# One small operation moved from GpSimd to VectorE, and an activation table loaded earlier, in a fused attention and experts kernel

## The chip, the core and the metric

The kernel runs on one core of one Trainium2 chip. The metric is the device time of one execution in microseconds (us). A core has five engines that work side by side, each with a queue of its own that it works off in order: TensorE (PE, matrix products; PEld is its weight load), VectorE (DVE), ScalarE (ACT, functions from a table that is loaded in sets), GpSimd (POOL) and SyncE (SP, which issues most of the DMAs). An instruction waits at the head of its queue until the semaphores that it names are up, and all behind it wait with it.

## The reference, cut to what matters

Three parts run one after the other on 3072 tokens of 384 channels: a gated linear attention, a layer of eight experts of which each token takes at most one, and a gated feed-forward layer behind a root mean square.

```python
# attention, per batch and head, over t
state = f[t] * state + outer(k[t], v[t]);  y[t] = q[t] @ state
# experts: tokens with x @ w_skip > 0 only
h = np.maximum(xc[mask] @ w1[e], 0.0)
y[mask] = gate_w[mask, None] * (h @ w2[e])
out[do_compute] = xc + y
# gated feed-forward
rms = np.sqrt(np.mean(x * x, axis=-1, keepdims=True) + 1e-06)
xn = x / rms * rms_g
g = xn @ w_gate
silu = g * (1.0 / (1.0 + np.exp(-g)))
return (silu * (xn @ w_val)) @ w_out
```

## The kernel before, in words

**Numbers.** Products run in 16 bits: every operand is split into a high and a low part, and three products of parts are added in PSUM. The splits are made on the chip: ScalarE writes the high part (L390, L414), VectorE or GpSimd the low one (L391, L416). Activations carry a scale of 512 (`SX`).

**Stages.** Attention takes the first 180 us or so: 24 tiles of 128 tokens, each routed to its expert's rows in a DRAM table `xs` by an indirect scatter. Then come the eight experts, up to some 335 us. Expert `e` reads its 256 rows transposed, and for each of eight blocks `m` of the hidden layer makes nine products into PSUM (`products`, L993), the relu's high part on ScalarE (`hh`, L996) and its low part on VectorE (`hl`, L997), and, two blocks later (`LAG`), six products of the second layer (L1040). Last comes the gated layer: `pair` for the first two blocks of 512 tokens, `block` for the other four. Its `up` makes nine gate products (`pwg`) and nine value products (`pwv`, both L846), takes Silu of the gate on ScalarE (`sg`, L850) and multiplies on VectorE (`hf`, L852); `down` (L869) multiplies by the output weights.

**Side work in the expert stage.** Between the blocks of an expert run pieces of other work, dealt by `steps` out of two queues of generators: preparing the weights of the next experts (`prep1`, `prep2`) and of the gated layer (`prep_in`, with `narrow`, L190 to L197, which turns 64-bit values into 32-bit ones, then L409, L414, L416), and treating rows that leave the experts or skip them. The latter is what the change touches. `square` forms x2 from an expert's output and its input (L446 on VectorE and L447 on GpSimd, or L444 on GpSimd alone), lets ScalarE square it and sum the squares along the row (L451), then computes on GpSimd first mean plus epsilon (L452) and then its power -0.5 (L453), and scales the row by that: the high part on ScalarE (L457), the low part on VectorE (L458). `place` then scatters the row into the DRAM table `xnd` (L477, an indirect DMA that GpSimd issues); `first` transposes it straight into the input of the first two blocks. `square` runs 30 times: 16 tiles of expert rows, 6 of `middle` and 8 of `first`. Sums of squares also go into `ms_x`, from which `bounds` checks near the end that no row is too small (L930).

**Order.** The program fixes a priority for every instruction by where it is written; the order on each engine's queue is then made at build time by a planner that simulates the engines with modelled durations (`schedule_with_timeline_sim=True`). `tc.issue_after(a)` holds what is written in its block behind instruction `a` on the same engine. `pins` collects the two relu instructions of each block; `run` uses the newest of them to hold side work back. The tables of functions are loaded once at the start, for exponential and logarithm (L763), and once when the first Silu comes (L850); the second load is put there when the program is built.

The functions that the change touches, with the line numbers of the profile:

Of the kernel before, what the change touches and what calls it, by code (L numbers as in the profile page):

```python
# [13 lines left out]
AF = mybir.ActivationFunctionType  # L14
ALU = mybir.AluOpType
# [5 lines left out]
SX = 2.0 ** 9  # L21
# [62 lines left out]
def fused_kernel(ctx, tc, q, k, v, f, w_skip, w_gate, w1, w2, g_gate, g_val, g_out, rms_g, out, dbg=None):  # L84
    nc = tc.nc
    B, H, S, D = q.shape
    DM = H * D
# [42 lines left out]
    ms_x = keep.tile([128, 2 * E + MID + 2 * NB], F32, name="ms_x")  # L130
# [214 lines left out]
    def bank(i):  # L345
        return {"tag": "bt", "bufs": 2} if i in (1, 2) else {"tag": f"b{i}", "bufs": 1}
# [87 lines left out]
    def halves(t):  # L434
        return t[:, 0:DM].bitcast(F16)

    def parts(t):
        return halves(t).rearrange("p (a d) -> p a d", a=2)

    def square(xr, idx, y=None):  # L440

        x2 = nk.tile([128, DM], F32, tag="x2", name="x2")
        if y is None:
            nc.gpsimd.tensor_tensor(out=x2, in0=parts(xr)[:, 0, :], in1=parts(xr)[:, 1, :], op=ALU.add)  # L444
        else:
            nc.vector.scalar_tensor_tensor(out=x2, in0=y, scalar=xr[:, DM:DM + 1], in1=parts(xr)[:, 0, :], op0=ALU.mult, op1=ALU.add)  # L446
            nc.gpsimd.tensor_tensor(out=x2, in0=x2, in1=parts(xr)[:, 1, :], op=ALU.add)  # L447
        yield
        junk = nk.tile([128, DM], F32, tag="junk", name="junk", bufs=1)
        m = nk.tile([128, 3], F32, tag="m2", name="m2", bufs=4)  # L450
        nc.scalar.activation(out=junk, in_=x2, func=AF.Square, accum_out=m[:, 0:1])  # L451
        nc.gpsimd.tensor_scalar(out=m[:, 1:2], in0=m[:, 0:1], scalar1=1.0 / DM, scalar2=1e-6 * SX * SX, op0=ALU.mult, op1=ALU.add)  # L452
        nc.gpsimd.tensor_tensor(out=m[:, 2:3], in0=m[:, 1:2], in1=mhalf[:, 0:1], op=ALU.pow)  # L453
        yield
        xn = nk.tile([128, ROW], F32, tag="xn", name="xn")
        xp = parts(xn)
        nc.scalar.activation(out=xp[:, 0, :], in_=x2, func=AF.Copy, scale=m[:, 2:3])  # L457
        nc.vector.scalar_tensor_tensor(out=xp[:, 1, :], in0=x2, scalar=m[:, 2:3], in1=xp[:, 0, :], op0=ALU.mult, op1=ALU.subtract)  # L458
        yield
        return xn, m  # L460

    def place(xr, idx, y=None):

        xn, m = yield from square(xr, idx, y)
        mt = xr[:, DM:]
        if y is None:
            ms = m[:, 0:1]
        else:
            junk = nk.tile([128, DM], F32, tag="junk", name="junk", bufs=1)
            m3 = nk.tile([128, 1], F32, tag="m3", name="m3")  # L470
            nc.scalar.activation(out=junk, in_=parts(xr)[:, 0, :], func=AF.Square, accum_out=m3)
            ms = m3
        nc.vector.scalar_tensor_tensor(out=ms_x[:, idx:idx + 1], in0=mt[:, 1:2], scalar=0.0, in1=ms, op0=ALU.is_equal, op1=ALU.max)
        nc.vector.tensor_copy(out=xn[:, DM:], in_=mt)
        at = nk.tile([128, 1], I32, tag="at", name="at")
        nc.vector.tensor_scalar(out=at, in0=mt[:, 1:2], scalar1=float(NONE), scalar2=None, op0=ALU.add)
        sc = nc.gpsimd.indirect_dma_start(out=xnd, out_offset=bass.IndirectOffsetOnAxis(ap=at.bitcast(U32), axis=0), in_=xn, in_offset=None,  # L477
                                          bounds_check=NTOK - 1, oob_is_err=False)
        for o in places:
            tc.declare_no_dep(sc.ins, o, reason="the rows of two scatters differ")  # L480
        places.append(sc.ins)
        yield
# [432 lines left out]
    def bounds():  # L915
        NBIG = 2 + 2 * E + 3
        NC = 3 + NBIG
        NA = NC + 2 * E + 1
        bad = keep.tile([128, NC], F32, name="bad")
        vio = keep.tile([128, 4], F32, name="vio")  # L920
        tot = keep.tile([1, NA + NT], F32, name="tot")

        def worst(j, a, op, lim, red):

            nc.vector.tensor_reduce(out=vio[:, j:j + 1], in_=a, axis=AX.X if len(a.shape) == 2 else AX.XY, op=red)
            nc.vector.tensor_scalar(out=bad[:, j:j + 1], in0=vio[:, j:j + 1], scalar1=lim, scalar2=None, op0=op)

        worst(0, dec, ALU.is_le, DECAY, ALU.max)
        worst(1, ex_sum, ALU.is_le, EXPSUM, ALU.max)
        worst(2, ms_x, ALU.is_ge, 1.0, ALU.min)  # L930
        nc.vector.tensor_scalar(out=bad[:, 3:NC], in0=big, scalar1=TINY, scalar2=None, op0=ALU.is_ge)
        pt = ps.tile([128, 512], F32, **bank(3), name="tot")
        nc.tensor.matmul(pt[:, 0:NC], lhsT=onef, rhs=bad, start=True, stop=True)
        nc.tensor.matmul(pt[:, NC:NA], lhsT=ones, rhs=cnt, start=True, stop=True)

        def beyond(lo, hi, least, most=None):
            o, a = tot[:, lo:hi], pt[0:1, lo:hi]
            if most is None:
                nc.vector.tensor_scalar(out=o, in0=a, scalar1=least, scalar2=None, op0=ALU.is_lt)
            else:  # L940
                mid = (least + most) / 2.0
                nc.vector.tensor_scalar(out=o, in0=a, scalar1=-mid, scalar2=None, op0=ALU.add)
                nc.vector.tensor_tensor(out=o, in0=o, in1=o, op=ALU.mult)
                nc.vector.tensor_scalar(out=o, in0=o, scalar1=(most - mid) ** 2, scalar2=None, op0=ALU.is_gt)

        beyond(0, 3, 127.5)
        beyond(3, NC, 0.5)
        beyond(NC, NC + E, LOW, CAP)
        beyond(NC + E, NC + E + 1, NSK + 256, NSK + 128 * MID)
        beyond(NC + E + 1, NA, float(RA))  # L950
        return tot, NA
# [20 lines left out]
    pins = []  # L972
# [39 lines left out]
    def expert(e):  # L1012
        w2h, w2l = W[e][2:4]
        c0 = 0
        if e in ahead:
            xT, h = ahead.pop(e)
            c0 = RA
        else:
            xT = ek.tile([128, 2 * KD, CAP], F16, tag="exT", name="exT")
        rows(e, xT, c0, CAP, NT)  # L1020
        xr = nk.tile([128, CAP // 128, ROW], F32, tag="exr", name="exr", bufs=ERB)
        after(nc.sync.dma_start(out=xr, in_=xs[e * CAP:(e + 1) * CAP, :].rearrange("(t p) c -> p t c", p=128)), scatters)
        py = [ps.tile([128, DM], F32, **bank(4 + 2 * (e % 2) + t), name=f"ey{t}") for t in range(CAP // 128)]
        hs = {}

        def up(m):
            ph = ps.tile([128, 1, CAP - c0], F32, **bank(m % 4), name="ph")
            products(e, xT, ph, (m,), c0, CAP)
            if c0:
                hs[m] = [a[:, m, :] for a in h]  # L1030
            else:
                hs[m] = [ek.tile([128, CAP], F16, tag="h" + a, name="h" + a, bufs=LAG + 2) for a in "hl"]
            relu(hs[m][0][:, c0:CAP], hs[m][1][:, c0:CAP], ph[:, 0, :])

        def down(m):
            hh, hl = hs.pop(m)
            for t in range(CAP // 128):
                sl = slice(t * 128, (t + 1) * 128)
                for j, (a, w) in enumerate(((hh, w2h), (hh, w2l), (hl, w2h))):
                    nc.tensor.matmul(py[t], lhsT=a[:, sl], rhs=w[:, m, :], start=(m == 0 and j == 0), stop=(m == KF - 1 and j == 2))  # L1040

        for m in range(KF + LAG):
            if m < KF:
                up(m)
            if m >= LAG:
                down(m - LAG)
            yield
        for t in range(CAP // 128):
            add(place(xr[:, t, :], 2 * NB + MID + 2 * e + t, py[t]), ("y", e), 1)
# [24 lines left out]
    def run(main, n):  # L1074
        for _ in main:
            a, b = pins[-PIN]
            with tc.issue_after(a), tc.issue_after(b):
                for r in (0, 1):
                    steps(n[r], r)
# [19 lines left out]
    with m1x:  # L1099
        for e in range(E):  # L1100
            need("a", e)
            need("e", e)
            run(expert(e), N2)
            if e + WB < E:
                add(prep1(e + WB), ("a", e + WB))
                add(prep2(e + WB), ("e", e + WB))
            if e < MID:
                add(middle(e), ("mid", e), 1)
            if 2 <= e < 6:
                for t in (0, 1):  # L1110
                    a = 2 * (e - 2) + t
                    add(first(a // NB, a % NB), ("b", a // NB), 1)
        gates(0, 6)
# [58 lines left out]
```

## Time and profile before

| what | value |
|---|---|
| median of 3 runs | 774.69 us (773.26 to 774.88) |
| the profiled execution's own time | 774.52 us |
| its span, first to last instruction | 772.8 us |
| mean granted TensorE clock | 0.977 |
| busy: TensorE, VectorE, ScalarE, GpSimd | 719.5, 417.7, 362.7, 216.1 us |
| L451, squares of x2, ScalarE, x30 | 15.5 us, 518 ns each |
| L452, factor and epsilon, GpSimd, x30 | 13.8 us, 459 ns each |
| L453, power, GpSimd, x30 | 24.4 us, 814 ns each |
| table loads, ScalarE, x2 | 1283 ns each |

The profiled execution is 1.7 us longer than its span, which counts from the first instruction to the last. Durations are those of one execution. A row of a group gives line, engine, operation, output and inputs, shape and count, then busy time and mean duration, then how long the engine stood idle in front of these instructions and what ended that. An idle engine costs nothing unless the end of the kernel waits for it.

### The profile page before, as it was taken

How to read it: one execution, taken by the hardware profiler on the slowest of the kernel's cores; microseconds unless marked ns; L12 is line 12 of the kernel's file. 1: busy time of each engine (PE TensorE's matmuls, PEld its weight loads, DVE VectorE, ACT ScalarE, POOL GpSimd, SP SyncE). 2: the span in 40 equal slices, each digit the busy share in tenths (PEclk: the TensorE clock that was granted, in tenths of full speed). 3: DMA queues.
4: the chain of work that ended last, by engine and by line, in shares of the span. 5: the costliest groups of instructions: out<-in, count | busy, mean ns of one | idle time of the engine just before them, and what ended most of it. 6: DMA issues, size and time to landing. Idle time of an engine off the chain costs nothing.

```text
span 772.8 us, 14043 instructions
## 1 busy us (share of the span) xinstructions
PE 719.5 (93%) x5452; PEld 442.8 (57%) x5452; DVE 417.7 (54%) x879; ACT 362.7 (47%) x803; POOL 216.1 (28%) x286
## 2 busy tenths in 40 slices
PE   8999798995999888769999999999999999999995
PEld 5788687784776655534444566455455455555443
DVE  2788386885688888999999700222222222222230
ACT  5887477643577667778766410222312222123131
POOL 5221742442165565677320010200100020002002
PEclk9999899997999999999999999999999999999998
DMA  9999887844778998754332400100200030001001
GB/s 153 178 198 198 209 160 182 231 142 131 217 250 241 265 263 259 237 154 150 110 123 82 82 22 20 42 1 1 62 20 1 1 83 0 1 1 42 1 0 46
DMA packets 166459, 88.10 MB, mean 114 GB/s; under 512 B 137432, under 2 KB 151048, under 8 KB 166384
## 3 DMA queue, kind: packets, MB, share of 16 engines
q1 hardware_dynamic: 161904, 74.44, 39.9%
q0 software_dynamic: 4480, 12.67, 4.5%
q8 instruction: 45, 0.74, 0.4%
q14 instruction: 30, 0.25, 0.1%
HBM read 64.18 MB, written 16.24 MB: 104 GB/s over the span
## 4 chain that ended last, share of the span: by engine, by line
PE 67%; DVE 9%; DMA 8%; ACT 5%; POOL 4%; issue 4%; SPq 2%; POOLq 0%; ACTq 0%; DVEq 0%
PE po L869 18%; PE pwv L846 18%; PE pwg L846 18%; DMA st<-in_moe_w_dram 3%; PE py L641 2%; DMA xnd<-xn,at 2%; PE sc L625 2%; DVE w2l L391 2%; SPq L557 1%; PE py L636 1%; DVE w1l L391 1%; PE ptq L607 1%; DVE xn L458 1%; DVE hl L997 1%; DMA st<-in_moe_w_gate_dram 1%
## 5 line engine op out<-in xcount | busy, mean ns | idle before, releaser
L852 DVE SCALAR_TENSOR_TENSOR hf<-pwv,sg 128x512 f32<-128x512 f32 x72 | 49.5, 689 | 181.4 <-PE pwv L846 181.4
L877 POOL DMA_INDIRECT out_dram<-ot,ids x24 | 23.7, 988 | 336.8 <-ACT ot L876 332.3
L846 PE MATMUL pwg<-xnT,wgh 128*128 128x512 f16 x432 | 106.3, 382 | 7.5 <-ACT sg L850 7.5
L846 PE MATMUL pwv<-xnT,wvh 128*128 128x512 f16 x432 | 105.6, 379 | 0.0
L855 ACT CAST gh<-hf 128x512 f16<-128x512 f32 x72 | 44.3, 615 | 108.5 <-DVE hf L852 108.3
L869 PE MATMUL po<-wol,gh 128*128 128x384 f16 x288 | 93.7, 326 | 0.0
L869 PE MATMUL po<-woh,gh 128*128 128x384 f16 x288 | 93.7, 326 | 0.0
L869 PE MATMUL po<-woh,gl 128*128 128x384 f16 x288 | 93.4, 326 | 0.0
L850 ACT ACTIVATE sg<-pwg 128x512 f32<-128x512 f32 x72 | 42.5, 593 | 101.4 <-PE pwg L846 101.4
L869 PEld LDWEIGHTS <-gh 128*128 128x128 f16 x576 | 56.4, 98 | 41.8
L846 PEld LDWEIGHTS <-wgh 128*128 128x128 f16 x432 | 42.5, 98 | 55.4 <-issue 8.9
L856 DVE TENSOR_TENSOR gl<-hf,gh 128x512 f16<-128x512 f32 x72 | 52.6, 731 | 35.4 <-ACT gh L855 35.4
L846 PEld LDWEIGHTS <-wvh 128*128 128x128 f16 x432 | 42.3, 98 | 50.4 <-issue 0.3
L993 PE MATMUL ph<-exT,w1h 128*128 128x256 f16 (+1 forms) x384 | 57.3, 276 | 8.5 <-DMA exT<-xs 8.5
L846 PE MATMUL pwg<-xnT,wgl 128*128 128x512 f16 x216 | 59.3, 381 | 0.0
L846 PE MATMUL pwv<-xnT,wvl 128*128 128x512 f16 x216 | 58.7, 379 | 0.0
L993 PEld LDWEIGHTS <-w1h 128*128 128x128 f16 x432 | 40.6, 101 | 19.9 <-DMA exT<-xs 8.6
L1040 PE MATMUL ey<-w2h,hh 128*128 128x384 f16 x112 | 37.0, 331 | 7.1 <-ACT hh L996 7.1
L588 POOL TENSOR_TENSOR qs<-q,ep 128x384 f32<-128x384 f32 x24 | 26.8, 1117 | 56.3 <-ACT ep L584 38.5
L876 ACT ACTIVATE ot<-po 128x384 f32<-128x384 f32 x24 | 11.6, 489 | 58.2 <-PE po L869 50.9
L869 PEld LDWEIGHTS <-gl 128*128 128x128 f16 x288 | 28.2, 98 | 18.6
L1040 PE MATMUL ey<-w2h,hl 128*128 128x384 f16 x112 | 31.4, 332 | 7.1 <-DVE hl L997 5.2
(203 smaller groups left out, 1396.0 us busy)
## 6 DMA issues: line engine op xcount, KB each, us to landing
st<-in_moe_w_dram SPq DMA_DIRECT2D x32, 768.0 KB, 6.3
f<-in_f_logit_dram SPq DMA_DIRECT2D x24, 192.0 KB, 4.6
q<-in_q_dram SPq DMA_DIRECT2D x24, 192.0 KB, 4.0
k<-in_k_dram SPq DMA_DIRECT2D x24, 192.0 KB, 4.6
v<-in_v_dram SPq DMA_DIRECT2D x24, 192.0 KB, 4.4
st<-in_moe_w_gate_dram SPq DMA_DIRECT2D x6, 768.0 KB, 4.6
st<-in_moe_w_val_dram SPq DMA_DIRECT2D x6, 768.0 KB, 4.6
st<-in_moe_w_out_dram SPq DMA_DIRECT2D x6, 768.0 KB, 4.3
```

The costliest lines, as they stand in the source:

```text
L391: nc.vector.scalar_tensor_tensor(out=lo[:, :, sl], in0=src[:, :, sl], scalar=scale, in1=hi[:, :, sl], op0=ALU.mult, op1=ALU.subtract)
L588: nc.gpsimd.tensor_tensor(out=qs[:, :, 0:D], in0=ins["q"], in1=ep, op=ALU.mult)
L625: nc.tensor.matmul(scs[r][:, j, :], lhsT=T["k"][64 * r:64 * r + 64, j, :], rhs=T["q"][64 * r:64 * r + 64, j, :], start=True, stop=True)
L846: nc.tensor.matmul(p, lhsT=w, rhs=x, start=(j == 0), stop=(j == len(terms) - 1))
L850: nc.scalar.activation(out=sg, in_=pg, func=AF.Silu, scale=1.0 / SG)
L852: nc.vector.scalar_tensor_tensor(out=hf, in0=pv, scalar=SH / SG, in1=sg, op0=ALU.mult, op1=ALU.mult)
L855: nc.scalar.copy(out=hh, in_=hf)
L856: nc.vector.tensor_tensor(out=hl, in0=hf, in1=hh, op=ALU.subtract)
L869: nc.tensor.matmul(po[t], lhsT=a[:, sl], rhs=w, start=(m == 0 and j == 0), stop=(m == KF2 - 1 and j == 2))
L877: sc = nc.gpsimd.indirect_dma_start(out=out, out_offset=bass.IndirectOffsetOnAxis(ap=at[:, t:t + 1].bitcast(U32), axis=0), in_=ot, in_offs ...
L993: nc.tensor.matmul(out[:, i, :], lhsT=a, rhs=r, start=(j == 0), stop=(j == len(terms) - 1))
L1040: nc.tensor.matmul(py[t], lhsT=a[:, sl], rhs=w[:, m, :], start=(m == 0 and j == 0), stop=(m == KF - 1 and j == 2))
```

## The change

Four edits. The sum of squares is divided by the row length inside Square, by a scale of 384 to the power -0.5, here and in the second square that `place` makes for the check. What is left of L452, the addition of epsilon, goes to VectorE. The check's limit is divided by the row length. And the set of functions that holds Silu is loaded by hand, written behind expert one's work (`e == 0`) and held behind its last relu on ScalarE.

```diff
@@ square
-        nc.scalar.activation(out=junk, in_=x2, func=AF.Square, accum_out=m[:, 0:1])
-        nc.gpsimd.tensor_scalar(out=m[:, 1:2], in0=m[:, 0:1], scalar1=1.0 / DM, scalar2=1e-6 * SX * SX, op0=ALU.mult, op1=ALU.add)
+        nc.scalar.activation(out=junk, in_=x2, func=AF.Square, scale=DM ** -0.5, accum_out=m[:, 0:1])
+        nc.vector.tensor_scalar(out=m[:, 1:2], in0=m[:, 0:1], scalar1=1e-6 * SX * SX, scalar2=None, op0=ALU.add)
         nc.gpsimd.tensor_tensor(out=m[:, 2:3], in0=m[:, 1:2], in1=mhalf[:, 0:1], op=ALU.pow)
@@ place
-            nc.scalar.activation(out=junk, in_=parts(xr)[:, 0, :], func=AF.Square, accum_out=m3)
+            nc.scalar.activation(out=junk, in_=parts(xr)[:, 0, :], func=AF.Square, scale=DM ** -0.5, accum_out=m3)
@@ bounds
-        worst(2, ms_x, ALU.is_ge, 1.0, ALU.min)
+        worst(2, ms_x, ALU.is_ge, 1.0 / DM, ALU.min)
@@ the loop over experts
             run(expert(e), N2)
+            if e == 0:
+                with tc.issue_after(pins[-1][0]):
+                    nc.scalar.preload_act_table_set("silu_and_others")
             if e + WB < E:
                 add(prep1(e + WB), ("a", e + WB))
```

## The prediction

> **What bounds the kernel now.** I read the page first (span, TensorE's busy tenths), then busy time by stage, then TensorE's waits, the timelines around its longest one, and last the chain of waits that leads there.
>
> ```profile
> span 772.8 us, 14043 instructions
> PE   8999798995999888769999999999999999999995
> ```
>
> A digit of the second row is 19.3 us. From slice 19 on, about 360 us, TensorE is full until the last slice: there the gate and value products bound, and nothing the change touches is late. The holes that can be won or lost lie before. By stage:
>
> ```profile
> core 0: us, PE busy (x) PEld busy (x) DVE busy (x) ACT busy (x) POOL busy (x), PEclk, DMA share, GB/s
> 320.00:340.00 20.00, 17.31 (x107) 10.33 (x108) 19.92 (x32) 13.73 (x33) 16.97 (x15) 1.00 0.77 253
> 340.00:360.00 20.00, 12.56 (x51) 5.38 (x51) 18.22 (x30) 13.99 (x27) 15.10 (x16) 0.83 0.44 126
> ```
>
> Columns after the length: busy time of TensorE, its weight loads, VectorE, ScalarE, GpSimd. At the end of the expert stage VectorE is full (19.92 of 20), and TensorE waits. The table of waits of that stage (us in total, times, longest) names for whom:
>
> ```profile
> PE pwg L846 <- ACT sg L850: 7.5, 1, 7.5
> PE ey L1040 <- ACT hh L996: 7.1, 7, 2.3
> PE ey L1040 <- DVE hl L997: 5.2, 7, 2.4
> ```
>
> One wait of 7.5 us for the first gate function, and 14 of about one each for an expert's relu. The timelines, ScalarE's and then TensorE's, show the long one (start, us, engine, line):
>
> ```profile
> 343.16 0.51 ACT L409 ACTIVATE fb<-fb,gsc 128x256 f32<-128x256 f32 x1 [2.10 <-DVE fb L197]
> ...
> 344.88 0.60 ACT L457 ACTIVATE xn<-x,m 128x384 f16<-128x384 f32 x1
> 345.49 1.28 ACT L850 ACT_TABLE_LOAD   x1
> 346.79 0.60 ACT L850 ACTIVATE sg<-pwg 128x512 f32<-128x512 f32 x1
> ```
> ```profile
> 347.44 1.01 PE L846 MATMUL pwg<-xnT,wgh 128*128 128x512 f16 x2 [7.53 <-ACT sg L850]
> ```
>
> sg's row has no bracket, so it waited for nothing but its place in ScalarE's queue: behind weight and row work (L409, L457), and last behind the table load. It ends at 347.39 and TensorE starts 0.05 us later. So this load is on the path, whole.
>
> **The change, part by part.** The profiled execution took 774.52 us, 1.72 over its span, beside a median of 774.69 for the runs shown; the sum is made against 774.52.
>
> *The table load moved.* Gone from between 345.49 and 346.79: -1.28 us. By the order in the program it comes behind expert one's last relu:
>
> ```profile
> 201.24 0.30 ACT L996 ACTIVATE eah<-ph 128x160 f16<-128x160 f32 x1 [1.29 <-PE ph L993]
> 201.44 1.57 ACT L390 ACTIVATE w2h<-st 128x768 f16<-128x768 f32 x2
> 204.17 0.38 ACT L996 ACTIVATE hh<-ph 128x256 f16<-128x256 f32 x1 [1.17 <-PE ph L993]
> ```
>
> ```profile
> 200.00:220.00 20.00, 20.00 (x156) 14.66 (x155) 15.33 (x37) 14.29 (x32) 9.61 (x12) 1.00 0.67 202
> ```
>
> There two weight splits are queued behind it and then expert two's first relu, in front of which ScalarE idles 1.17 us: the load fits but for 0.1 us, and TensorE, 20.00 busy of 20 in this stretch, consumes that relu only two blocks of products later. I take 0; without that cover it is 1.28 again, at most. What is late next at the gate is TensorE's need for VectorE, 18.22 busy of 20 in that stage, but VectorE's own products there wait on the same ScalarE queue, so I let the whole 1.28 through; the bounds are 0 and 1.28. The Trainium skill, "ScalarE: Activation LUTs", section "What ACT_TABLE_LOAD costs", gives a switch 1283 ns and about 1380 ns of drain. The load agrees; no drain shows (the operation before ends at 345.48, sg starts at 346.79), and by the page's 2.66 the total would be 772.3.
>
> *The add moved from GpSimd to VectorE, the division into Square's scale.* Square with a constant other than one costs nothing by these two rows of 128x512, the first with a scale and the second without:
>
> ```profile
> L645 ACT ACTIVATE xT<-py 128x512 f16<-128x512 f32 x24 | 14.1, 586 | 1.1 <-PE py L641 1.0
> L610 ACT COPY Tq<-ptq 128x512 f32<-128x512 f32 x24 | 14.0, 585 | 6.2 <-PE ptq L607 6.1
> ```
>
> The limit in the bounds check is a constant, 0 too. The 30 GpSimd operations of L452 go. Most of their time is beside other work: GpSimd waits for ScalarE before them. What counts are those on the chain from 188 to 348 us, five pieces:
>
> ```profile
> L452 POOL TENSOR_SCALAR m<-m x30: 190/394/1222, 207.9 to 362.2; 128x1 f32<-128x1 f32 x30
> ```
> ```profile
> 214.56 0.80 POOL m L452
> ...
> 331.73 0.38 POOL m L452
> ```
>
> With 0.19, 0.27 and 0.80 between these two, together 2.44 us. In their place come five adds on VectorE. The trace has none; the nearest rows are a tensor_scalar of the same size and a copy of four elements; the other two are what such an add would find running:
>
> ```profile
> L476 DVE TENSOR_SCALAR at<-exr x16: 136/142/155, 207.1 to 360.8; 128x1 int32<-128x1 f32 x16
> ```
> ```profile
> L474 DVE COPY xn<-exr 128x4 f32<-128x4 f32 x16 | 6.4, 398 | 1.8 <-DMA xnT<-xn 1.8
> ```
> ```profile
> L997 DVE SCALAR_TENSOR_TENSOR hl<-ph,hh 128x256 f16<-128x256 f32 x56 | 22.9, 415 | 2.1 <-ACT hh L996 2.0
> ```
> ```profile
> L391 DVE SCALAR_TENSOR_TENSOR w2l<-st,w2h 128x768 f16<-128x768 f32 x27 | 28.5, 1074 | 5.3 <-ACT w2h L390 5.2
> ```
>
> An add takes 142 to 398 ns; I take 142, the same operation at the same size: 5 x 0.142 = 0.71. Each may find VectorE in the middle of something: nothing at best, a whole weight split of 1.07 us at worst; I take half of one relu's low part, 0.2 each, 1.0 together. So this term is -2.44 + 0.71 + 1.0 = -0.73, between -2.44 + 0.71 = -1.73 and -2.44 + 5 x (0.398 + 1.074) = +4.9. The Trainium skill, "Advanced Engine Details and Errata", section "VectorE Performance Modes", says that GpSimd's instructions and two-port VectorE ones block each other, and counts tensor_scalar among those with such a mode: a rule against this move. The rows bear it out for wider ones (below), but the 16 of one element never exceeded 155 ns, so by the trace the add is not held.
>
> The other 25 adds occupy VectorE for 25 x 0.142 = 3.6 us (9.9 at 398 ns). How much reaches the end I read from the lines of VectorE that the chain from 188 to 348 names: 8.3 + 6.3 + 5.5 + 4.9 = 25%.
>
> ```profile
> by line: DMA xnd<-xn,at 10.0%; issue 8.3%; DVE w2l L391 8.3%; DMA st<-in_moe_w_dram 7.8%; DVE w1l L391 6.3%; DVE xn L458 5.5%; DVE hl L997 4.9%; DMA st<-in_moe_w_gate_dram 4.5%; PE ph L993 4.5%; POOL m L453 3.4%; PE ey L1040 3.3%; ACT w2h L
> ```
>
> That is +0.9 (up to 2.5).
>
> *The new wait.* VectorE's add waits for ScalarE's sum of squares; behind it in VectorE's queue stand hl, for which TensorE waits, and the weight splits. GpSimd's power waits for the add; behind it stand the adds of x2 and the row scatters. The first row shows what GpSimd loses to this wait now, the other two what VectorE loses to its like:
>
> ```profile
> POOL m L452 <- ACT junk L451: 21.4, 16, 3.1
> ...
> DVE xn L458 <- ACT xn L457: 6.0, 8, 2.4
> ...
> DVE ms_x L473 <- ACT junk L471: 0.5, 1, 0.5
> ```
>
> L473 reads the same kind of accumulator: 0.5 us for 16 of them, 0.9 for 30. A third of it on the path is +0.3; the upper end is L458's 6.0. GpSimd's 21.4 is that of an engine that arrives early, which VectorE, 19.92 busy of 20, seldom does. Sum: -1.28 - 0.73 + 0.9 + 0.3 = -0.8, that is 773.7 us.
>
> **The rivals.** The order on the engines comes from a planner that fills queues by modelled times, so with 30 operations on another engine the order after 207 us may be dealt anew. Three of the rivals turn on that.
>
> *The long wait shrinks by more.* It is 7.5 us because of one collision, VectorE first and GpSimd under it:
>
> ```profile
> 329.73 0.55 DVE L192 TENSOR_SCALAR fb<-fb 128x768 f32<-128x768 f32 x1
> ```
> ```profile
> 336.67 3.87 DVE L192 TENSOR_SCALAR fb<-fb 128x768 f32<-128x768 f32 x1
> ```
> ```profile
> 336.74 0.92 POOL L444 TENSOR_TENSOR x<-xr 128x384 f32<-128x384 f16 x1
> 337.60 0.92 POOL L447 TENSOR_TENSOR x<-x,exr 128x384 f32<-128x384 f32 x1
> 338.47 1.64 POOL L416 TENSOR_TENSOR wgl<-fb,wgh 128x768 f16<-128x768 f32 x1
> ```
>
> The same operation took 0.55 us alone and 3.87 beside three GpSimd operations in a row, and L409 on ScalarE waited behind it. If the adds fall elsewhere, 3.3 us go besides; sg's queue would then be held by the two powers before its rows, which are GpSimd's and remain. Of the 3.3 I let 2.5 through: 773.7 - 2.5 = 771.2 us. Were the rest of the wait to go as well (7.5 - 1.28 - 3.3 = 2.9), it would be 768.3. For it: an accident of this size is not likely to be met again in a new order. Against: the same three GpSimd operations remain.
>
> *The next wait takes the table's place* (no change): VectorE is late at the gate, sg's consumer or the freeing of a PSUM bank holds TensorE where sg did. Without the 1.28 the sum is +0.5: 775.0.
>
> *Slower: VectorE stalls in front of the adds.* If ScalarE's Square comes later than planned (it waits for GpSimd's x2, itself held by VectorE), the add stands at the head of a full VectorE queue and hl with it, and TensorE's 5.2 us for hl grow. Without any stall the sum is -1.1; with 6.0 us of it on the path it is +4.9, or 779.4; with two thirds, 4.0, it is 777.4. It decides from 2.7 us on the path, where the sum reaches 1.6.
>
> *The change does not do what it says*: if a function used behind the early load were missing from its set, loads would multiply, 1.28 us each, over the relus of the seven experts that follow. Behind the one load of the gate function Square already runs with no second load,
>
> ```profile
> 348.00 0.53 ACT L451 ACTIVATE junk<-x 128x384 f32<-128x384 f32 x1
> ```
>
> but relu does not occur behind it. Two such loads on the path would bring -0.8 + 2.6 = +1.8, 776.3 or more.
>
> **How the numbers follow.** About 0.2%, or 1.55 us, is what a measurement of this kernel can tell from no change. The forecast has 0.42, with a range of its own from 771.9 to 775.5; of that 0.15 lies beyond 1.55 us of gain. The larger gain has 0.25, the next wait 0.08, the stall 0.23, the loads 0.02. Faster: 0.15 + 0.25 = 0.40; same: 0.27 + 0.08 = 0.35; slower: 0.23 + 0.02 = 0.25. The range takes in the larger gain but for its end, 768.5, and the stall's case up to between its two prices, 778.5.
>
> **What would show it.** Right: one table load near 202 us and none before the first sg; TensorE's wait for sg down to about 6 us; L452 on VectorE at some 0.14 us with waits for ScalarE under 1 us; powers starting sooner after Square. Wrong: waits of VectorE for junk L451 of several us, more than 5.2 us of TensorE waiting for hl, a third table load, or the same 7.5 us under another name, such as hf or x of VectorE.

## The result, and the profile after

| | before | after |
|---|---|---|
| median of the runs | 773.98 us (4 runs) | 780.39 us (4 runs, 779.09 to 784.57) |
| the profiled execution's own time | 774.52 us | 779.09 us |
| its span | 772.8 us | 777.4 us |
| VectorE busy | 417.7 us, x879 | 412.3 us, x909 |
| GpSimd busy | 216.1 us, x286 | 208.2 us, x256 |

The change makes the kernel slower: the ratio is 1.011, with a 95% interval from 1.0083 to 1.0136 (the two medians of the table alone are 0.83%, 6.4 us, apart). The profiled execution of after is the fastest of its four, so its trace shows 4.6 us of the loss. Of the runs below, e3 has one execution of 4112 us and e7 one of 928, which their medians count and their ratios leave out. The prediction said 773.7 us, and its range ended at 778.5.

The page of the kernel after, first its span and TensorE's busy tenths:

```profile
span 777.4 us, 14054 instructions
PE   8999798995998898959999999999999999999995
```

From slice 19 on it is full again, so the 4.6 us of span were lost ahead of some 375 us. Busy time by stage (length; busy time of TensorE, weight loads, VectorE, ScalarE, GpSimd; the granted clock):

```profile
320.00:340.00 20.00, 15.81 (x100) 9.57 (x101) 17.55 (x40) 12.79 (x31) 14.41 (x12) 1.00 0.78 251
340.00:360.00 20.00, 12.71 (x45) 5.06 (x45) 18.04 (x28) 13.78 (x31) 12.88 (x11) 0.74 0.39 101
```

VectorE, 19.92 of 20 before, is now 17.55: it has not become the bound, it stands idle more. TensorE's granted clock from 340 to 360 us is 0.74 instead of 0.83. The table of TensorE's waits from 188 to 348 us (us in total, times, longest):

```profile
PE ey L1040 <- DVE hl L997: 8.2, 5, 2.8
PE pwg L846 <- ACT sg L850: 7.7, 1, 7.7
PE ey L1040 <- ACT hh L996: 2.7, 3, 1.5
```

The wait for hl went from 5.2 to 8.2 us, with fewer and longer waits; that for hh fell from 7.1 to 2.7; that for sg stayed, though the table load is no longer ahead of it. In sum TensorE is no more idle in this window than before (busy 138.84 us of 160, before 137.53), but its mean granted clock there is 0.93 instead of 0.96. ScalarE's timeline shows the load in its new place (L1106 is its new line), and the first Silu:

```profile
201.24 1.28 ACT L1106 ACT_TABLE_LOAD   x1
202.53 0.38 ACT L996 ACTIVATE hh<-ph 128x256 f16<-128x256 f32 x1
...
343.69 1.30 ACT L409 ACTIVATE fb<-fb,gsc 128x256 f32<-128x256 f32 x3 [2.79 <-DVE fb L197]
344.90 0.57 ACT L850 ACTIVATE sg<-pwg 128x512 f32<-128x512 f32 x1
```

The load is hidden, as said. The 7.5 us (7.7 here) have another cause under the same name: L409 waited 2.79 us for VectorE's L197, which stood behind an L195 of 3.59 us (0.95 in the median of its 18), beside GpSimd's L444 and L416. That is the collision of before with another victim:

```profile
339.07 3.59 DVE L195 SCALAR_TENSOR_TENSOR fb<-st,fb 128x768 int32<-128x768 int32 x1
```

**The adds.** The view of line 452, with its duration (least, median, most), what its engine waited for, and who waited for it:

```profile
L452 DVE TENSOR_SCALAR m<-m x30: 138/142/151, 206.4 to 371.2; 128x1 f32<-128x1 f32 x30
its engine sat idle before it (us, times) until:
who waited for it (us, times):
  POOL m L453: 16.5, 7
...
```

The list under the second line is empty: VectorE never waits for ScalarE in front of an add. It is the other way round. From the end of Square's sum (the READ_ACCUMULATOR rows) to the start of its add there are 1.7 us on average and 3.6 at most, over 1 us in 18 of 30 rows, because the add stands in VectorE's queue behind other work. GpSimd waits: 16.5 us for adds, and 12.0 and 4.6 more for L473 and L496, which follow them in VectorE's queue; together 33.1 us in front of the power, where before it had 21.4 in front of L452. For a row this means 3.25 us on average from the end of the sum to the end of its power, where before it was 2.29.

**Where TensorE loses it.** The first new hole, a stretch in which TensorE stands idle, lies at 237 us. TensorE's row, and VectorE's timeline ahead of it:

```profile
236.83 0.82 PE L1040 MATMUL ey<-w2h,hl 128*128 128x384 f16 x2 [2.72 <-DVE hl L997]
```
```profile
231.37 0.21 DVE L146 TENSOR_REDUCE big<-w1h 128x1 f32<-128x64 f16 x1
236.09 0.17 DVE L474 COPY xn<-xr 128x4 f32<-128x4 f32 x1 [4.50 <-issue]
236.16 0.15 DVE L476 TENSOR_SCALAR at<-xr 128x1 int32<-128x1 f32 x1
236.23 0.14 DVE L452 TENSOR_SCALAR m<-m 128x1 f32<-128x1 f32 x1
236.29 0.15 DVE L473 SCALAR_TENSOR_TENSOR ms_x<-xr,m 128x1 f32<-128x1 f32 x1
236.35 0.42 DVE L997 SCALAR_TENSOR_TENSOR hl<-ph,hh 128x256 f16<-128x256 f32 x1
```

VectorE stood 4.50 us in front of L474, a copy of four elements into a buffer of xn, and behind it stood the add, and hl, which TensorE needs. There are two such buffers; the copy must wait until an earlier row's scatter has landed from the same one. (The profile finds no releaser here and writes "issue"; but the scatter issued at 229.69 landed 6.3 us later, at 236.0, and the copy starts at 236.09.) In before the same copy and hl pass at once:

```profile
233.09 0.16 DVE L474 COPY xn<-xr 128x4 f32<-128x4 f32 x1
233.29 0.42 DVE L997 SCALAR_TENSOR_TENSOR hl<-ph,hh 128x256 f16<-128x256 f32 x1
```

because that scatter (L477 on GpSimd) had been issued 2.0 us earlier, at 227.69 instead of 229.69, and had landed in 5.0 us instead of 6.3. Why it was issued earlier, ScalarE's timelines tell, first before, then after; the last row of each is GpSimd's scatter:

```profile
225.87 0.61 ACT L457 ACTIVATE xn<-x,m 128x384 f16<-128x384 f32 x1 [0.38 <-POOL m L453]
226.65 0.83 ACT L390 ACTIVATE w1h<-st 128x768 f16<-128x768 f32 x1
...
227.69 1.07 POOL L477 DMA_INDIRECT xnd<-xn,at  x1 [0.70 <-DVE xn L458]
```
```profile
226.60 0.84 ACT L390 ACTIVATE w2h<-st 128x768 f16<-128x768 f32 x1 [2.54 <-DMA st<-in_moe_w_dram]
227.85 0.60 ACT L457 ACTIVATE xn<-x,m 128x384 f16<-128x384 f32 x1
...
229.69 1.67 POOL L477 DMA_INDIRECT xnd<-xn,at  x1 [0.18 <-issue]
```

The row's power ended at 225.84 us in before and at 225.86 in after, so it is not that. Before, the row's scaling L457 stands ahead of the weight splits; after, it stands behind one (L390) that waits 2.54 us for its weights to arrive. The planner, which simulates the engines, has dealt the row's steps further back. I take it that a step on a third engine made the row look later to it; e9 below, where the row's chain stays as it was, has no hole here. At 258.40 us the same happens again: VectorE stands 4.63 us in front of L474, TensorE 2.85 for hl.

A hole can cost more than its length. TensorE around the first one (busy time, then granted clock):

```profile
234.00:236.00 2.00, 0.11 (x1) 0.85 1.03 388
236.00:238.00 2.00, 1.17 (x5) 0.50 0.50 130
238.00:240.00 2.00, 2.00 (x9) 0.50 1.04 249
240.00:242.00 2.00, 2.00 (x10) 0.50 0.49 115
242.00:244.00 2.00, 2.00 (x17) 0.94 0.79 258
```

The clock is at half for 6.8 us, from 235.4 to 242.2, and 5.4 us of it are work, of which half, 2.7, is lost: this hole costs about twice its length. It is not so of each: the one at 258 us, 2.85 long, brought 3.4 us of half clock, and a wait of 2.43 us in before, at 322 us, brought none. The stage makes good a part of this later, where before waits and after does not: the ninth of the 66 instructions on L997 (the last of them are hl) comes 1.8 us earlier than in before and the last but one 0.5 later, so 2.3 us are lost here. Over 200 to 450 us TensorE stood idle 24.2 us instead of 21.8, and ran at half clock for 23.9 us instead of 10.2 (sums over stretches of 2 us; a part of the half-clock time is idle time).

**And at the end of the expert stage.** VectorE's L446 takes an expert's rows out of PSUM and frees the bank for the gate and value products. The fourth last, before and after:

```profile
335.81 0.62 DVE L446 SCALAR_TENSOR_TENSOR x<-ey,exr 128x384 f32<-128x384 f32 x1
```
```profile
347.81 0.61 DVE L446 SCALAR_TENSOR_TENSOR x<-ey,exr 128x384 f32<-128x384 f32 x1
```

It is 12.0 us late, the other three 7 to 9. So TensorE had made three whole products when it came to wait for sg, after the change two, and it waits again at 354.26 (1.76 us) and at 375.11 (1.27 us). From 375 us to the end the kernel after is 4.6 us behind and stays so; 4.1 of them, from 0.5 to 4.6, are this stage's.

### The profile page after: what moved, and what is told of

Read it like the earlier page. It is cut to its first block, busy times and chain, and to the rows that moved or that the text cites. A ratio compares the mean times of both kernels' runs of the same rounds, so it can differ in the third digit from the quotient of the medians.

```text
span 777.4 us, 14054 instructions
## 1 busy us (share of the span) xinstructions
PE 721.6 (93%) x5452; PEld 444.5 (57%) x5452; DVE 412.3 (53%) x909; ACT 363.9 (47%) x803; POOL 208.2 (27%) x256
## 4 chain that ended last, share of the span: by engine, by line
PE 62%; DVE 10%; issue 8%; DMA 8%; POOL 5%; ACT 5%; SPq 2%; POOLq 0%; ACTq 0%; DVEq 0%
PE po L869 18%; PE pwg L846 16%; PE pwv L846 16%; DMA xnd<-xn,at 4%; PE py L641 2%; SPq L557 1%; PE sc L625 1%; PE ph L993 1%; DVE w2l L391 1%; DMA xnT<-xn 1%; DVE w1l L391 1%; POOL xs L738 1%; PE py L636 1%; PE ey L1040 1%; POOL qs L588 1%
## 5 line engine op out<-in xcount | busy, mean ns | idle before, releaser
L846 PE MATMUL pwg<-xnT,wgh 128*128 128x512 f16 x432 | 107.7, 386 | 10.7 <-ACT sg L850 8.9
L993 PE MATMUL ph<-exT,w1h 128*128 128x256 f16 (+1 forms) x384 | 59.1, 278 | 8.7 <-DMA exT<-xs 8.7
```

Source lines behind the costliest of these rows:

```text
L846: nc.tensor.matmul(p, lhsT=w, rhs=x, start=(j == 0), stop=(j == len(terms) - 1))
L993: nc.tensor.matmul(out[:, i, :], lhsT=a, rhs=r, start=(j == 0), stop=(j == len(terms) - 1))
```

## The experiments

Each ran beside kernel before on the same chip; ratios are to that, with 95% intervals.

### One part at a time

Theory A: the adds stand in VectorE's queue and make the powers, and with them the rows, late. Theory B: the early load makes the build deal the order anew, and that costs.

**e1, the load alone**, against before:

```diff
+            if e == 0:
+                with tc.issue_after(pins[-1][0]):
+                    nc.scalar.preload_act_table_set("silu_and_others")
```

> The early table load alone; mean and epsilon stay one GpSimd operation. Theory A (the adds in VectorE's queue make the powers on GpSimd late): 772 to 774 us, nothing lost, up to 1.3 us won. Theory B (the load makes the planner deal a new order to all engines from 207 us on, and that order has the worse collisions; the adds are innocent): about 780 us, as the whole change.

772.28 us, ratio 0.9994 (0.9976 to 1.0012): no loss, so theory B falls, and no gain that can be told, though one of 1.28 us (0.17%) lies inside the interval. The load was whole on TensorE's path before; where are its 1.28 us? TensorE's timelines, first before, then e1:

```profile
347.44 2.72 PE L846 MATMUL pwg<-xnT,wgh 128*128 128x512 f16 x6 [7.53 <-ACT sg L850]
349.95 1.26 PE L846 MATMUL pwg<-xnT,wgl 128*128 128x512 f16 x3
351.05 1.24 PE L846 MATMUL pwv<-xnT,wvh 128*128 128x512 f16 x5
```
```profile
345.20 2.72 PE L846 MATMUL pwg<-xnT,wgh 128*128 128x512 f16 x6 [6.12 <-ACT sg L850]
347.72 1.48 PE L846 MATMUL pwg<-xnT,wgl 128*128 128x512 f16 x3
349.00 2.48 PE L846 MATMUL pwv<-xnT,wvh 128*128 128x512 f16 x6
```

The wait is 1.41 us shorter and work resumes 2.24 us earlier (0.83 of it had come about ahead of the wait). But six matmuls take 2.72 us at half clock instead of 1.46, and the clock comes back at 350.9 us in before and at 351.1 in e1. e1 only makes more of its products at half speed: pwg and the pwv behind it take 6.76 us in place of 5.55. Of the 1.41 us that the wait gave, the clock took 1.21, in this pair of traces; one pair does not show that it is always so.

**e2, the add and the scale without the load**, against after:

```diff
-            if e == 0:
-                with tc.issue_after(pins[-1][0]):
-                    nc.scalar.preload_act_table_set("silu_and_others")
```

> The adds on VectorE and the scale in Square, the table where it was before. Theory A: about 781 us, slower than before by 6 to 8 us, with GpSimd's powers waiting over 20 us for VectorE. Theory B: 773 to 775 us, no change.

782.49 us, 1.0139 (1.0118 to 1.0159), some 10.7 us where theory A had 6 to 8: the whole loss is here, and the powers wait for VectorE as A said, 33 us.

**e3, the scale alone**: as e2, but the addition stays on GpSimd:

```diff
-        nc.vector.tensor_scalar(out=m[:, 1:2], in0=m[:, 0:1], scalar1=1e-6 * SX * SX, ...)
+        nc.gpsimd.tensor_scalar(out=m[:, 1:2], in0=m[:, 0:1], scalar1=1e-6 * SX * SX, ...)
```

> Only the scale in Square and the limit of the check; the add stays on GpSimd, and the order of the instructions is that of before on every engine. Both theories: 774 us, no change within 0.2%. Anything else means that Square's scale or GpSimd's second operation on the number has a price, which neither theory has.

774.75 us, 1.0018 (0.9993 to 1.0043): no change, so what e2 shows is the add's.

**e4, the add on ScalarE**, behind the Square that it reads; the rest as after:

```diff
-        nc.vector.tensor_scalar(out=m[:, 1:2], in0=m[:, 0:1], scalar1=1e-6 * SX * SX, ...)
+        nc.scalar.activation(out=m[:, 1:2], in_=m[:, 0:1], func=AF.Copy, bias=1e-6 * SX * SX)
```

> The whole change, but the add on ScalarE, right behind the sum that it reads, so that no queue but ScalarE's own stands between the sum and GpSimd's power. Theory A: 773 to 776 us, most of the loss gone, GpSimd's wait in front of the powers under 15 us. Theory B: about 780 us, since the load is where the change puts it.

771.78 us, 0.9988 (0.9969 to 1.0007): no loss with the add on ScalarE. But the other half of A's expectation fails: GpSimd waits 34.9 us for the adds in front of the powers, more than the 33.1 of after, so the sum of these waits is not what costs. From the end of the sum to the end of its power a row takes 2.28 us here, as in before. TensorE's wait in front of the gate products is 2.9 us, for L446 and no longer for sg, and that brings nothing either: its trace has two holes of 3.4 and 4.4 us for hh in the expert stage instead. VectorE's order is dealt anew here too (below), so this run alone does not tell the add's place from the order that it brings.

### Buffers, and which rows

Theory C: the longer chain makes the rows fall behind since only two can be on their way, and they keep their PSUM banks too long at the end. Theory D: each add's own wait in line is paid, whatever the buffers.

**e5 and e6, three buffers** for before and for after:

```diff
-        x2 = nk.tile([128, DM], F32, tag="x2", name="x2")
+        x2 = nk.tile([128, DM], F32, tag="x2", name="x2", bufs=3)
...
-        xn = nk.tile([128, ROW], F32, tag="xn", name="xn")
+        xn = nk.tile([128, ROW], F32, tag="xn", name="xn", bufs=3)
```

> The kernel before, with three buffers instead of two for the two tiles of a row that is on its way (x2, the row's sum, and xn, the normalised row); nothing else. It is the control for the next run. Theory C (the adds make each row's chain longer, and since only two rows can be on their way the rows fall behind and keep their PSUM banks too long at the end of the expert stage): before has little of this backlog, so 769 to 774 us, at most some 3 us faster than before. Theory D (each add's own wait in VectorE's queue is paid on the path, some 1.7 us for each of a handful of rows, whatever the buffers): the buffers change nothing here, 771.5 to 774.

> The whole change, with three buffers instead of two for x2 and xn. Theory C: the loss goes, within 2 us of the control with three buffers, so 769 to 775 us. Theory D: the loss stays, 778 to 782 us.

e5: 766.09 us, 0.9905 (0.9868 to 0.9942), more of a gain than either theory gave it. e6: 770.21 us, 0.9959 (0.9936 to 0.9982). The change still costs 0.5%, 4.1 us, half of what it cost; the two intervals just overlap. C has the one half: L446 of the last four tiles comes 13 to 18 us earlier than in before, and the waits in front of the gate products are gone. The other half lies at the two holes of 237 and 258 us, which e6 still has, and no longer makes good: its last hl but one is 4.0 us later than e5's. TensorE's waits from 225 to 262 us, and VectorE's row ahead of the first:

```profile
PE ey L1040 <- DVE hl L997: 7.9, 2, 4.0
```
```profile
235.03 0.15 DVE L476 TENSOR_SCALAR at<-xr 128x1 int32<-128x1 f32 x1 [4.29 <-DMA xnd<-xn,at]
```

The copy finds its third buffer, but three instructions on L476 writes a scatter's row numbers (at), of which there are still two buffers, and stands 4.29 us for the landing of the scatter that uses the other. hl is behind it again.

**e7 and e8, the add on VectorE for the first 15 rows and for the last 15**; in the others GpSimd adds (against after, `nth` counts the rows):

```diff
-        nc.vector.tensor_scalar(out=m[:, 1:2], in0=m[:, 0:1], scalar1=1e-6 * SX * SX, ...)
+        eng = nc.vector if nth < 15 else nc.gpsimd
+        eng.tensor_scalar(out=m[:, 1:2], in0=m[:, 0:1], scalar1=1e-6 * SX * SX, ...)
```

> The whole change, but VectorE adds for the first 15 of the 30 rows only; the other 15 rows leave this one addition to GpSimd as before. Theory C: the backlog of the early rows is worked off before the last experts, so the loss goes, 771 to 775 us. Theory D: the loss goes by rows, so about half of it, 775 to 778 us.

> The other half: GpSimd adds for the first 15 rows, VectorE for the last 15. Theory C: all of the loss is here, since these rows are the ones that keep the PSUM banks, 778 to 782 us. Theory D: half of it, 775 to 778 us.

e7: 779.0 us, 1.0079 (1.0053 to 1.0104). e8: 775.95 us, 1.0032 (1.0008 to 1.0057). C had put all into the late rows, and there it is wrong: the early ones cost more. e7 has both holes (2.81 and 2.77 us), e8 has neither. D expected 775 to 778 us of each; e8 is there, e7 over it.

### Who waits, and the order

**e9, an add that nobody waits for**, in before, beside GpSimd's own two operations. Theory F: the adds cost by being in VectorE's queue.

```diff
         nc.scalar.activation(out=junk, in_=x2, func=AF.Square, accum_out=m[:, 0:1])
+        nc.vector.tensor_scalar(out=spare, in0=m[:, 0:1], scalar1=1e-6 * SX * SX, ...)
```

> The kernel before with one more VectorE operation behind each Square: the same 128x1 addition on the same accumulator value, into a tile that nobody reads; GpSimd keeps both its operations. VectorE's queue then holds the 30 adds of the change, but the power does not wait for them. Theory C (what costs is that GpSimd's power waits for an add that stands in line in VectorE's queue): no change, 771 to 775 us. Theory F (the adds cost by being in VectorE's queue: their time, the order that is dealt anew around them): the loss stays, 778 to 783 us.

781.72 us, where before had 776.0: 1.0073 (1.0047 to 1.0098). The holes at 237 and 258 us are not there, as C says; but more than half of the loss is. C does not explain it.

**e10 and e11, a third buffer for at too**, in before and in after:

```diff
-        at = nk.tile([128, 1], I32, tag="at", name="at")
+        at = nk.tile([128, 1], I32, tag="at", name="at", bufs=3)
```

> The kernel before with three buffers for x2 and xn and also for at, the row numbers of a scatter; the control for the next run. At the time of the first control or a little under, 763 to 767 us, by every theory.

> The whole change with three buffers for x2, xn and at. With three for x2 and xn alone the profile still showed TensorE waiting 3.9 and 4.0 us at 235 and 257 us for an hl that stood in VectorE's queue behind at L476, which waited for the landing of a scatter that had gone out late. Theory C: with a third at these two waits fall under 1 us each and most of the 4 us between change and control goes: 764 to 768 us, within 2 us of the control. Theory F: what is left has nothing to do with that buffer, 769 to 772 us, 3 to 5 us over the control.

e10: 768.81 us, 0.9903 (0.9881 to 0.9925). e11: 768.92 us, 0.9897 (0.9869 to 0.9924). Both lie above the times expected, on a chip where before is slower too (776.0); between them there are 0.1 us. Now the change costs nothing, and C's step at the two holes is shown: TensorE's waits in the same stretch of e11 are

```profile
PE ey L1040 <- ACT hh L996: 2.8, 3, 1.9
PE ey L1040 <- DVE hl L997: 0.9, 2, 0.6
```

where e6 had 7.9 us for hl. The adds of e11 still start 1.15 us after their sums on average, so a wait in line is not by itself a price.

**e12, a version of the change that is faster**: e4 with the three buffers.

```diff
-        x2 = nk.tile([128, DM], F32, tag="x2", name="x2")
+        x2 = nk.tile([128, DM], F32, tag="x2", name="x2", bufs=3)
...
-        nc.vector.tensor_scalar(out=m[:, 1:2], in0=m[:, 0:1], scalar1=1e-6 * SX * SX, ...)
+        nc.scalar.activation(out=m[:, 1:2], in_=m[:, 0:1], func=AF.Copy, bias=1e-6 * SX * SX)
```

> The whole change with its addition on ScalarE, directly behind the Square that it reads, and three buffers for x2, xn and at. Theory C: no add stands in VectorE's queue, so it is at the control or under it, 761 to 767 us. Theory F says the same; the run is to see whether a version of the change is faster than both kernels.

766.92 us, 0.9886 (0.9862 to 0.9910): faster than both kernels. Nearly all of that is the buffers' (e10 has 0.9903, the intervals overlap).

**e13 to e16, time or order?** e9's adds leave 87 of the 1234 other instructions in VectorE's queue at another place, the change 159; the load alone moves hardly any, the scale none. F1: the adds cost by their time. F2: by the order that is dealt anew. e13 is e9 for 26 rows, whose adds together leave the order nearly as it was; e14, e15 and e16 are e9 for one row only.

```diff
+        if nth in ROWS: nc.vector.tensor_scalar(out=spare, in0=m[:, 0:1], ...)
```

> The kernel before with an addition that nobody waits for behind 26 of the 30 Squares; the four rows left out are those whose addition alone makes the build deal the queues anew. Of the 1234 other instructions of VectorE's queue three stand at another place than before (87 in the run with 30 such adds, 159 in the change). Theory F1 (the 30 adds cost by their time in VectorE's queue): 26 of 30 of that run's loss stay, 0.5 to 0.7%. Theory F2 (they cost because the order of the queue is dealt anew around them): no change, within 0.25% of before.

> One single addition of 0.14 us that nobody waits for, behind the Square of row 26; 58 of VectorE's 1234 other instructions stand at another place. Theory F1: 0.14 us cannot be measured, no change. Theory F2: a change of some 0.2 to 0.8% either way is possible, since the place of the last experts' instructions moves.

> The same with one addition behind the Square of row 21: 63 instructions moved, and as with the 30 adds the VectorE operation that frees the first of the last four PSUM banks now stands behind the last hl instead of ahead of it. Theory F1: no change. Theory F2: slower, 0.3 to 0.8%, if it is this place that the 30 adds changed.

> The same with one addition behind the Square of row 14: 68 instructions moved; the first of the last four freeing operations keeps its place ahead of the last hl, the other three stand one weight split further back. Theory F1: no change. Theory F2: a change that can be measured, of either sign, less than for row 21 if the first freeing operation is the one that matters.

| run | adds | others moved | us | ratio |
|---|---|---|---|---|
| e9 | 30 | 87 | 781.72 | 1.0073 (1.0047 to 1.0098) |
| e13 | 26 | 3 | 775.05 | 1.0030 (1.0006 to 1.0054) |
| e14 | 1 | 58 | 773.72 | 1.0002 (0.9983 to 1.0021) |
| e15 | 1 | 63 | 777.55 | 1.0056 (1.0034 to 1.0078) |
| e16 | 1 | 68 | 775.68 | 1.0032 (1.0014 to 1.0049) |

One add of 0.14 us in the right row costs 0.56%, 4.3 us; in another row it costs nothing. Time cannot do that: F2 holds. How many instructions move says nothing of the price: of the 879 that VectorE's trace shows, 102 fall out of the order of before in the change (counted against the longest common order), but 92 do in e4, 105 in e5 and 108 in e10, and none of these is slower. e13 lies between the two theories, so part of its 0.3% may be the adds' time; its interval leaves that open. One place is the same in e9 and e15. VectorE in before, then VectorE and GpSimd in e15:

```profile
326.88 0.94 DVE L195 SCALAR_TENSOR_TENSOR fb<-st,fb 128x768 int32<-128x768 int32 x1
```
```profile
327.05 3.52 DVE L195 SCALAR_TENSOR_TENSOR fb<-st,fb 128x768 int32<-128x768 int32 x1
330.56 0.41 DVE L997 SCALAR_TENSOR_TENSOR hl<-ph,hh 128x256 f16<-128x256 f32 x1
...
328.09 1.66 POOL L416 TENSOR_TENSOR wgl<-fb,wgh 128x768 f16<-128x768 f32 x1
```

The order now puts L195, a two-input operation on 768 columns, beside GpSimd's L444 and L416 (1.66 us, in the last row). It takes 3.52 us in place of 0.94, with an hl of the last expert and everything later behind it. e9 has the same row, 3.52 us at 328.66. In both, too, the fourth last L446 now stands behind the last hl (at 343.52 and 341.85 us), where before has it ahead (335.81); this is the place that e15's expectation named, and the two runs do not tell which of the two costs more. e16, where it stays ahead, costs 0.32%.

## Why the prediction was wrong

- **The load.** Its new place, its cover and its 1.28 us were right; "I let the whole 1.28 through" is not borne out. e1 gives -0.06% (-0.24 to +0.12), about -0.5 us, which can be told neither from 0 nor from -1.28. In e1's trace most of it went again, and not to another wait, as the rival had it, but to the clock.
- **The scale and the limit**: 0, as said (e3).
- **The five operations of L452, -2.44.** They are gone from GpSimd, but nothing came of it: the power follows on an add that comes later than they did.
- **The add's duration** was right (142 ns predicted and measured, 151 at most). By the rule of the Trainium skill, "Advanced Engine Details and Errata", section "VectorE Performance Modes", it might have been held; the 30 rows of the add say no. L195 is a scalar_tensor_tensor, which that section does not list; that it was held beside GpSimd is read from its row alone.
- **The step that failed**: "Each may find VectorE in the middle of something: ... I take half of one relu's low part, 0.2 each." That prices the instruction which runs when the add is ready. But a queue is worked off in order: the add waits for everything dealt ahead of it, and that waits for its own weights and buffers. Measured: 1.7 us on average, 3.6 at most. The terms of the add came to +0.5 us (-0.73 + 0.9 + 0.3); e2, which has the add and the scale alone, lost 10.7. And the sum counted five pieces of one chain in an order held fixed, while the order moved, and late rows are paid elsewhere: at the two holes by an hl that stands behind the buffer which a row frees too late.
- **The other 25 adds, +0.9 (up to 2.5).** e13, whose order is kept, has +2.3 us, between 0.5 and 4.2; no more can be said of their time.
- **The new wait of VectorE, and the slower rival.** Its time, 777.4 to 779.4, was nearest to the result by luck, since its mechanism did not happen: no idle time of VectorE in front of an add. The sign named for it, hl over 5.2 us, came for another reason.
- **The order dealt anew** was in the text, as what three of the rivals turn on, but the one collision that was priced was a gain: that of 3.87 us being dissolved. The runs show that the new order makes collisions as well (3.59 in after, 3.52 in e9 and e15), and of the three that moved it with one add none was faster, two were slower.
- **The large gain**, the wait for sg dissolved: in e4 it fell to 2.9 us and the time stayed.

Settled: the loss comes with the add on VectorE, and none that can be told with the load or the scale; the holes at 237 and 258 us come from scatters that land late while there are two buffers; the order alone can cost 0.56%. Open: how the 1.1% of the change divides between these, since after's order differs from before's by more than that of any one-add run; why the planner dealt the row's steps further back; how much of e13's 0.3% is time; and how much of the gain of the third buffers is their own, since they too bring a new order.

## What to carry to other kernels

An operation moved to a busy in-order engine costs the queue ahead of it, and it makes its own chain one engine longer: price it by who stands ahead of it and what those wait for, then look for the buffer that its chain frees and who stands behind that. Where the build orders the queues by a model, any edit that touches them draws a new order; an extra operation that nobody waits for shows how much a new order alone is worth, and a gain below that cannot be put down to the part. Give a chain that ends in a transfer one buffer more before shortening it by tenths of a microsecond: here that came with 1%, and the change was harmless.

## What the runs showed of the hardware

- TensorE's granted clock goes to 0.50 in whole pieces. In front of the gate products they are 6.8 us in before (344.0 to 350.9) and in e1, 10.2 us in after (341.2 to 351.5) and 3.4 us in e4. A wait of 2.72 us at 237 us was enough for 6.8 us of it, one of 2.85 at 258 us for 3.4, and one of 2.43 in before at 322 us brought none. The Trainium skill, "TensorE: Matmul & The Clock Gate", Part 1, gives a free-running window of some 3.4 us in which activity is judged, and lets the clock fall after an idle one; these lengths are one, two and three such windows, so the traces agree in that, but here a wait of 2.72 us, less than a window, was enough. So a shorter wait need not be a gain, as in e1's trace, and a short new one can cost twice its length.
- The same two-input operation of VectorE on 128x768 (L195) took 0.94 us in before and 3.52 to 3.59 beside two wide GpSimd operations. The 30 adds of one element stayed at 0.14 to 0.15 us, seven of them begun while GpSimd ran a sum, a weight split or a power; but L473, of one element and two inputs, took 1.44 us in after at 327.01, beside a scatter and L444.
